# State-major tokens and 32-outermost stores for the sread MLP, and a later place for the sums and sread of batch 1

## The chip, the cores and the metric

One core of one Trainium2 chip. The metric is the device time of one execution in microseconds (us); the kernel before takes 229.64 us (median of the 4 runs that were made beside the changed kernel). Times "at 43.9" are us from the start of the span of the profile in question. Every profile is of one execution. The *tail* is the time from the start of TensorE's last matmul to the end of the span; the *handoff* is the passage of TensorE from batch 0 to batch 1.

## The reference, cut to what matters

```python
# x: (8 batches, 8 heads, 512, 64), state: (8, 8, 32, 64)
a     = softmax(scale * x @ state.T)            # over the 32 states
xread = a @ state                               # 512 tokens of each batch
a2    = softmax(scale * state @ x.T)            # over the 512 positions
sread = a2 @ x                                  # 32 tokens of each batch
tokens = concat([xread, sread], axis=2)  ->  (8 * 544, 512)
out = silu(tokens @ w_in) @ w_out               # w_in (512, 2048), w_out (2048, 512)
```

So the output has 8 blocks of 544 rows of 2 KB. The first 512 rows of a block come from xread and the last 32 from sread. The sread rows of all batches (8 x 32 = 256 tokens) are computed together, last, in two tiles of 128 tokens.

## The kernel before

In short: for each batch, `scores` (TensorE) and `exps` (ScalarE) make the exponentials; `norm` (VectorE, GpSimd) makes `an`, whose transpose is `aT`; `w1_chunks` folds the state into `w_in` (the tile W1). G1 is `aT` times W1, followed by SiLU on ScalarE; G2 is the second matmul, of 4 token tiles `tt` with 16 steps `ft` each. The tile `es` holds the token sums and `sread` uses it. All of this is interleaved by hand; each engine runs its instructions in program order.

```python
xpool = ctx.enter_context(tc.tile_pool(name="xpool", bufs=2))   # x_nat: x of a batch, bf16
banks = ["a0", "a1", "a2", "a3"]          # 4 PSUM banks taken in turn by scores, w1_chunks, sread, ...
xmT = pers.tile([128, 2, 4, 128], BF16)   # sread tokens: [feature, tile, kt, token]
out_sread = out.rearrange("(bb s) m -> bb s m", s=544)
# ... (cut)
def token_sums(b):                        # VectorE only
    f = att.tile([128, 2, 4, NS], FP32, tag="es_f", name="es_f")
    es[b] = att.tile([128, 2, 2, 4, NS], BF16, tag="es", name="es")
    for hg in range(2):
        nc.vector.tensor_reduce(f[:, hg], exp_nat[b, hg].rearrange("p c s n -> p s n c"), axis=AX, op=ADD)
    nc.vector.tensor_copy(es[b][:, 0], f[:])
    nc.vector.tensor_tensor(es[b][:, 1], f[:], es[b][:, 0], op=SUB)

def sread(b):                             # 18 matmuls, then VectorE
    ps = bank([128, 2, 4, 2, NS], FP32, "ps_sr")
    # ... (cut) 2 matmuls ones x es[b]; 16 matmuls x_nat[b] x exp_nat[b]
    nc.vector.reciprocal(rb[:], ps[:, 1, :, :, :])
    for g in range(2):
        for u in range(2):
            rows, k2 = ds(64 * u, 64), ds(2 * g, 2)
            nc.vector.tensor_tensor(
                xmT[rows, b // 4, k2, ds(32 * (b % 4), 32)],
                ps[rows, 0, k2, u ^ g, :], rb[rows, k2, u ^ g, :], op=MULT)
# ... (cut)
def last_half(b, tt, half):               # the last 128 tokens, 256 columns at a time
    # ... (cut) 16 matmuls, copy to o
    nc.sync.dma_start(out_sread[ds(4 * tt, 4), ds(512, 32), cols], o[:])
# ... (cut) end of batch 0: its last tile
for ft in range(NFT):
    if ft == 5:  w1_chunks(1, (3,), (nc.scalar, nc.scalar))
    if ft == 11:
        pe_transpose_a(1, 0, nc.scalar); pe_transpose_a(1, 1, nc.vector)
        # ... casts of x of batch 2, load of batch 3, transpose of x of batch 2
    if ft == 4:  token_sums(1)
    if ft == 13: sread(1)
    if ft >= 14: upto(NFT + ft - 12)      # first G1 of batch 1
    G2(0, 3, ft)
upto(NFT + 4)
store(0, 3, nc.vector)
for b in range(1, B):                     # n = b + 1: the batch that is prepared
    for tt in range(4):
        for ft in range(NFT):
            at = (tt, ft)
            # (0, 12): scores, exps of n          (1, 0): norm of n, casts of x of n+1, load of x of n+2
            # (1, 8): token_sums(n)               (2, 8): w1_chunks(n, (0, 1), both)
            # (3, 1), (3, 3), ...: G1 of n        (3, 4): w1_chunks(n, (2, 3), both)
            # (3, 8): DMA transpose of x of n+1   (3, 10): sread(n)
            G2(b, tt, ft)
        store(b, tt, nc.scalar if tt in (1, 2) else nc.vector)
# sread MLP: 16 steps of G1, G2; store(B, 0); last_half(B, 1, 0); last_half(B, 1, 1)
```

The softmax here doesn't subtract the row's maximum and nothing guards it: scores larger than these inputs give would overflow.

Of the kernel before, what the change touches and what calls it, by code (L numbers as in the profile page):

```python
# [9 lines left out]
BF16 = mybir.dt.bfloat16  # L10
# [11 lines left out]
NS = 32  # L22
# [14 lines left out]
def kernel(  # L37
# [8 lines left out]
    nc = tc.nc  # L46
    ds = bass.ds
# [3 lines left out]
    pers = ctx.enter_context(tc.tile_pool(name="pers", bufs=1))  # L51
# [14 lines left out]
    def bank(shape, dtype, name):  # L66
        tag = banks[turn[0] % len(banks)]
        turn[0] += 1
        return psA.tile(shape, dtype, tag=tag, name=name)
# [8 lines left out]
    ones = pers.tile([128, 128], BF16)  # L78
    w_in_sb = pers.tile([128, 4, DF], BF16)
    w_out_sb = pers.tile([128, NFT, DM], BF16)  # L80
    xmT = pers.tile([128, 2, 4, 128], BF16)

    win_re = moe_w_in.rearrange("(kt p) f -> p kt f", p=128)
    wout_re = moe_w_out.rearrange("(gg q) m -> q gg m", q=128)
    out_re = out.rearrange("(n4 four) m -> n4 four m", four=4)
    out_sread = out.rearrange("(bb s) m -> bb s m", s=544)


    x_nat = {}
# [30 lines left out]
    def copy(eng, dst, src):  # L120
        if eng is nc.scalar:
            nc.scalar.activation(dst, src, func=COPY, bias=0.0)  # L122
        else:
            eng.tensor_copy(dst, src)  # L124
# [158 lines left out]
    def pe_transpose_a(b, hg, eng):  # L283
        ps = bank([128, 4, 128], BF16, "ps_at")
        for c in range(4):
            nc.tensor.transpose(ps[:, c, :], an[b, hg][:, c, :, :], ident[:])
        copy(eng, aT[b][:, hg, :, :], ps[:])
# [4 lines left out]
    def token_sums(b):  # L292
# [3 lines that stand above are left out]
            nc.vector.tensor_reduce(  # L296
                f[:, hg], exp_nat[b, hg].rearrange("p c s n -> p s n c"), axis=AX, op=ADD
            )
        nc.vector.tensor_copy(es[b][:, 0], f[:])  # L299
        nc.vector.tensor_tensor(es[b][:, 1], f[:], es[b][:, 0], op=SUB)  # L300
# [3 lines left out]
    def sread(b):  # L304
        ps = bank([128, 2, 4, 2, NS], FP32, "ps_sr")
        for part in range(2):
            nc.tensor.matmul(  # L307
                ps[:, 1, :, :, :],
                ones[:],
                es[b][:, part],  # L310
                start=(part == 0),
                stop=(part == 1),
                skip_group_check=True,
            )
        for kt in range(4):
            for c in range(4):
                nc.tensor.matmul(  # L317
                    ps[:, 0, kt, :, :],
                    x_nat[b][:, c, ds(2 * kt, 2), :],
                    exp_nat[b, kt // 2][:, c, ds(2 * (kt % 2), 2), :],  # L320
                    start=(c == 0),
                    stop=(c == 3),
                    skip_group_check=True,
                )
        rb = att.tile([128, 4, 2, NS], FP32, tag="rb", name="rb")
        nc.vector.reciprocal(rb[:], ps[:, 1, :, :, :])  # L326
        for g in range(2):
            for u in range(2):
                rows, k2 = ds(64 * u, 64), ds(2 * g, 2)
                nc.vector.tensor_tensor(  # L330
                    xmT[rows, b // 4, k2, ds(32 * (b % 4), 32)],
                    ps[rows, 0, k2, u ^ g, :],
                    rb[rows, k2, u ^ g, :],
                    op=MULT,
                )
# [27 lines left out]
    def w1_chunks(b, fbs, engs):  # L363
        w1_cols(b, [(512 * fb, 512) for fb in fbs], engs)
# [6 lines left out]
    def emit_G1(k):  # L371
        b, ft = divmod(k, NFT)
        ps = psH.tile([128, 512], FP32, tag="h1", name="h1")
        if b < B:
            for hg in range(2):
                nc.tensor.matmul(  # L376
                    ps[:],
                    W1[b][:, hg, ds(128 * ft, 128)],
                    aT[b][:, hg, :, :],
                    start=(hg == 0),  # L380
                    stop=(hg == 1),
                    skip_group_check=True,
                )
        else:
            for kt in range(4):
                nc.tensor.matmul(  # L386
                    ps[:, 0:256],
                    w_in_sb[:, kt, ds(128 * ft, 128)],
                    xmT[:, :, kt, :],
                    start=(kt == 0),  # L390
                    stop=(kt == 3),
                    skip_group_check=True,
                )
        n = 512 if b < B else 256
        g = gpool.tile([128, 512], BF16, tag="g", name="g")
        gt[k] = g
        nc.scalar.activation(g[:, 0:n], ps[:, 0:n], func=SILU, bias=0.0)
# [16 lines left out]
    def store(b, tt, eng):  # L414
        o = opool.tile([128, DM], FP32, tag="o_sb", name="o_sb")
        copy(eng, o[:], outs[tt][:])
        if b < B:
            nc.sync.dma_start(out_re[ds(136 * b, 128), tt, :], o[:])
        else:
            nc.sync.dma_start(out_sread[ds(4 * tt, 4), ds(512, 32), :], o[:])  # L420


    def last_half(b, tt, half):
        cols = ds(DM // 2 * half, DM // 2)
        ps = bank([128, DM], FP32, "o_half")
        for ft in range(NFT):
            nc.tensor.matmul(  # L427
                ps[:, 0 : DM // 2],
                gt[b * NFT + ft][:, ds(128 * tt, 128)],
                w_out_sb[:, ft, cols],  # L430
                start=(ft == 0),
                stop=(ft == NFT - 1),
                skip_group_check=True,
            )
        o = opool.tile([128, DM // 2], FP32, tag="o_half", name="o_half")
        copy(nc.vector, o[:], ps[:, 0 : DM // 2])
        nc.sync.dma_start(out_sread[ds(4 * tt, 4), ds(512, 32), cols], o[:])


    both = (nc.vector, nc.scalar)  # L440
# [2 lines left out]
    def upto(k):  # L443
        while done[0] < min(k, (B + 1) * NFT):
            emit_G1(done[0])
            done[0] += 1
# [72 lines left out]
    for ft in range(NFT):  # L519
        if ft == 5:  # L520
            w1_chunks(1, (3,), (nc.scalar, nc.scalar))
        if ft == 11:
            pe_transpose_a(1, 0, nc.scalar)
            pe_transpose_a(1, 1, nc.vector)
            for c in range(4):
                cast_x(2, nc.gpsimd, c, 1)
            load_x(3)
            transpose_x(2)
        if ft == 4:
            token_sums(1)  # L530
        if ft == 13:
            sread(1)
        if ft >= 14:
            upto(NFT + ft - 12)
        G2(0, 3, ft)
# [3 lines left out]
    for b in range(1, B):  # L539
        n = b + 1  # L540
        lead = 4 if b == 1 else 6
        for tt in range(4):
            for ft in range(NFT):
                at = (tt, ft)
                if tt == 0:
                    upto(NFT * b + min(lead + ft, NFT))
                if n < B:
                    if at == (0, NFT - lead):
                        scores(n, 0)
                        scores(n, 1)  # L550
                        exps(n, 0)
                        exps(n, 1)
                        nc.scalar.activation(warm[:], warm[:], func=SILU, bias=0.0)  # L553
                    if at == (1, 0):
                        for hg in range(2):
                            norm(n, hg)
                            transpose_a(n, hg)
                        if n + 1 < B:
                            for c in range(4):
                                cast_x(n + 1, nc.gpsimd, c, 1)  # L560
                        if n + 2 < B:
                            load_x(n + 2)
                    if at == (1, 8):
                        token_sums(n)
                    if at == (3, 8):
                        if n + 1 < B:
                            transpose_x(n + 1)
                    if at == (3, 10):
                        sread(n)
                    if at == (2, 8):  # L570
                        w1_chunks(n, (0, 1), both)
                    if at == (3, 4):
                        w1_chunks(n, (2, 3), both)
                    if tt == 3 and ft % 2 == 1 and ft // 2 < 6:
                        upto(NFT * n + ft // 2 + 1)
                elif tt > 0 and (ft % 3 == 2 or ft == NFT - 1):
                    upto(min(done[0] + 1, NFT * (B + 1)))
# [3 lines that stand above are left out]
            gt.pop(NFT * b + ft)  # L581
# [34 lines left out]
```

## Time and profile before

| | before |
|---|---|
| time, median of the 3 runs at hand then | 229.88 us |
| span of the profile | 228.3 us |
| TensorE (PE) busy | 213.5 us, 94% |
| start of the last matmul to end of span (the tail) | 7.4 us |

The page of the kernel before gives the span, and the busy time of each engine with its share of the span (PEld are the weight loads):

```profile
span 228.3 us, 3733 instructions
...
PE 213.5 (94%) x1462; PEld 102.4 (45%) x1488; DVE 103.2 (45%) x186; ACT 142.5 (62%) x241; POOL 45.8 (20%) x64
...
PE 88%; DVE 6%; issue 1%; ACT 1%; POOL 0%; POOLq 0%
```

The last line is the chain that ended last, by engine. It says that TensorE is what is waited for. (It shows no DMA; the landings of the last three stores are missing from this trace.) How much of it could go is not to be read from the 94%. The Trainium skill ("Perfetto Trace Analysis", section "Identifying the Most-Contended Engine") warns that matmul busy time is no good measure of the distance to the limit. What can be read is where TensorE stands still.

*The tail.* The windows of the kernel before give, for each stretch of one us, its length, the busy time of PE, PEld, DVE, ACT and POOL (with the count of instructions), the granted clock, the mean busy share of the 16 DMA engines, and what they moved in GB/s:

```profile
216.00:217.00 1.00, 1.00 (x6) 0.48 (x5) 0.00 (x0) 0.00 (x0) 0.00 (x0) 1.00 0.58 217
...
220.00:221.00 1.00, 1.00 (x12) 0.84 (x9) 0.00 (x0) 0.00 (x0) 0.00 (x0) 1.00 0.28 14
221.00:222.00 1.00, 0.22 (x2) 0.00 (x0) 0.42 (x1) 0.00 (x0) 0.00 (x0) 1.00 0.20 49
...
223.00:224.00 1.00, 0.00 (x0) 0.00 (x0) 0.00 (x0) 0.00 (x0) 0.00 (x0) 1.00 0.27 101
...
226.00:227.00 1.00, 0.00 (x0) 0.00 (x0) 0.00 (x0) 0.00 (x0) 0.00 (x0) 0.50 0.19 66
```

The last matmuls, in the timeline of the kernel before (start, duration; the tail is counted from the start of the last of the 32, 220.95):

```profile
217.56 3.66 PE L427 MATMUL o_half<-w_out_sb,g 128*128 128x256 bf16 x32
```

From 222 on nothing computes; the kernel waits for its last stores. An ordinary store (216 to 217) moves 217 GB/s. The sread stores move about 100 GB/s at a share of 0.27, which is about 4 of 16 engines.

*The end of batch 0.* The waits of TensorE in the kernel before (who waited for whom: us in total, times, longest):

```profile
PE ps_sr L307 <- DVE es L299: 1.2, 1, 1.2
...
PE ps_sr L307 <- DVE es L300: 0.5, 1, 0.5
```

And the timeline of the kernel before there (start, duration, engine, line, operation, output and inputs, shapes, count; in brackets the idle time before it and what ended it):

```profile
43.24 0.38 PE L405 MATMUL o<-w_out_sb,g 128*128 128x512 bf16 x1
43.35 0.60 ACT L122 ACTIVATE aT<-ps_at 128x512 bf16<-128x512 bf16 x1
...
44.83 0.28 PE L307 MATMUL ps_sr<-es,ones 128*128 128x256 bf16 x1 [1.21 <-DVE es L299]
...
45.57 0.27 PE L307 MATMUL ps_sr<-es,ones 128*128 128x256 bf16 x1 [0.45 <-DVE es L300]
...
46.35 0.59 PE L376 MATMUL h_664<-aT,W_400 128*128 128x512 bf16 x2
```

The `sread` matmuls (L307, L317) stand in TensorE's order ahead of the first G1 of batch 1 (L376) and wait for the sums. Of what the G1 needs, `aT` comes last; it is there from 43.95.

*VectorE at the norm of batch 2*, in the timeline of the kernel before:

```profile
60.91 0.25 DVE L267 RECIPROCAL rc<-rs 128x16 f32<-128x16 f32 x1
61.08 1.91 DVE L296 TENSOR_REDUCE es_f<-exp_nat 128x128 f32<-128x512 bf16 x2
63.02 0.70 DVE L299 CAST es<-es_f 128x256 bf16<-128x256 f32 x1
63.75 0.71 DVE L300 TENSOR_TENSOR es<-es_f,es 128x256 bf16<-128x256 f32 x1
64.39 0.68 DVE L124 CAST W_848<-ps_w_849 128x512 bf16<-128x512 f32 x1
```

The first W1 copy of batch 2 (L124) ends at 65.07. The first G1 of batch 2, which reads it, starts at 65.59 without a wait:

```profile
65.59 0.59 PE L376 MATMUL h_886<-aT,W_848 128*128 128x512 bf16 x2
```

VectorE is packed here, and only half a microsecond is to spare.

### The profile page before, as it was taken

The numbers are of one execution on the slowest core, as the hardware profiler recorded it, in microseconds if no ns is written. First come the engines' busy times: TensorE is split into PE (matmuls) and PEld (weight loads), VectorE is DVE, ScalarE is ACT, GpSimd is POOL, SyncE is SP. The second block draws the span as 40 slices with busy tenths as digits, with TensorE's granted clock in tenths as the row PEclk, the third lists the DMA queues.
The fourth block names the chain that finished last, engine by engine and source line by source line (L and its number), as shares of the span: only waits on it lengthen the run. The fifth ranks groups of instructions, "written<-read, shape, count | busy, mean of one in ns | idle before, by whom it ended". The sixth has DMA issues, their size and how long they took to land.

```text
span 228.3 us, 3733 instructions
## 1 busy us (share of the span) xinstructions
PE 213.5 (94%) x1462; PEld 102.4 (45%) x1488; DVE 103.2 (45%) x186; ACT 142.5 (62%) x241; POOL 45.8 (20%) x64
## 2 busy tenths in 40 slices
PE   7799899799999999999999999999999999999970
PEld 2534335344435443544354534444444444566550
DVE  5554946960765075516552565247434634100110
ACT  2555558679865985598558856885679477444110
POOL 8380001710450045003600260025001200000000
PEclk9999999999999999999999999999999999999997
DMA  6999974585169115911591159113611311111111
GB/s 191 184 196 196 204 226 140 184 199 126 51 128 275 56 48 130 284 46 50 112 296 51 49 121 283 61 46 92 141 47 46 95 46 46 46 49 41 51 24 68
DMA packets 33933, 26.97 MB, mean 118 GB/s; under 512 B 22012, under 2 KB 27900, under 8 KB 33916
## 3 DMA queue, kind: packets, MB, share of 16 engines
q1 hardware_dynamic: 27244, 15.21, 25.6%
q0 software_dynamic: 6672, 11.54, 22.6%
q8 instruction: 11, 0.18, 0.3%
q14 instruction: 6, 0.05, 0.1%
HBM read 17.30 MB, written 8.91 MB: 115 GB/s over the span
## 4 chain that ended last, share of the span: by engine, by line
PE 88%; DVE 6%; issue 1%; ACT 1%; POOL 0%; POOLq 0%
PE o L405 46%; PE ps_sc L244 2%; PE ps_sr L317 2%; PE o_half L427 2%; PE ps_xt L185 1%; PE ps_busy L130 1%; PE o_a L405 1%; DVE rs L266 1%; DVE es_f L296 1%; PE ps_sr L307 1%; DVE rb L326 1%; DVE W_214 L124 1%; ACT exp_nat L256 1%; ACT xT_143 L122 1%; DVE x_nat_141 L101 0%
## 5 line engine op out<-in xcount | busy, mean ns | idle before, releaser
L405 PE MATMUL o<-w_out_sb,g 128*128 128x512 bf16 x489 | 132.1, 380 | 0.5
L405 PEld LDWEIGHTS <-g 128*128 128x128 bf16 x528 | 50.0, 98 | 58.6 <-issue 7.1
L124 DVE COPY o_sb<-o 128x512 f32<-128x512 f32 x17 | 11.8, 692 | 64.4 <-PE o L405 64.1
L269 POOL TENSOR_TENSOR an<-exp_nat,rc 128x512 bf16<-128x512 bf16 (+1 forms) x16 | 15.9, 1009 | 111.2 <-DVE rc L267 111.0
L326 DVE RECIPROCAL rb<-ps_sr 128x256 f32<-128x256 f32 x8 | 14.1, 1758 | 16.6 <-PE ps_sr L317 16.6
L122 ACT ACTIVATE o_sb<-o 128x512 f32<-128x512 f32 x15 | 8.9, 596 | 13.5 <-PE o L405 5.3
L296 DVE TENSOR_REDUCE es_f<-exp_nat 128x128 f32<-128x512 bf16 x16 | 15.3, 1000 | 0.0
L266 DVE TENSOR_REDUCE rs<-exp_nat 128x16 f32<-128x512 bf16 x16 | 10.6, 660 | 2.2 <-ACT exp_nat L256 1.5
L96 POOL DMA_DIRECT2D x_f<-in_x_dram x7 | 6.5, 924 | 20.6 <-DVE x_nat_486 L101 19.1
L256 ACT ACTIVATE exp_nat<-ps_sc 128x512 bf16<-128x512 f32 x16 | 8.8, 595 | 1.1 <-PE ps_sc L244 1.0
L386 PEld LDWEIGHTS <-w_in_sb 128*128 128x128 bf16 x64 | 6.3, 98 | 3.9
L256 ACT ACT_TABLE_LOAD x6 | 7.7, 1283 | 0.1
L553 ACT ACT_TABLE_LOAD x6 | 7.7, 1283 | 0.1
L330 DVE TENSOR_TENSOR xmT<-ps_sr,rb 64x64 bf16<-64x64 f32 x32 | 7.1, 222 | 0.6
L350 PEld LDWEIGHTS <-stT 64*32 64x32 bf16 x264 | 2.8, 89 | 9.1 <-issue 8.5
L130 PE MATMUL ps_busy<-busy 128*128 128x512 bf16 x11 | 5.4, 627 | 1.4 <-DVE busy L144 1.2
L405 PE MATMUL o_a<-w_out_sb,g 128*128 128x512 bf16 x15 | 5.8, 396 | 0.1
L376 PEld LDWEIGHTS <-W_214 128*128 128x128 bf16 x32 | 3.2, 106 | 5.1 <-DVE W_214 L124 1.5
L300 DVE TENSOR_TENSOR es<-es_f,es 128x256 bf16<-128x256 f32 x8 | 5.1, 638 | 0.3
L376 PEld LDWEIGHTS <-W_400 128*128 128x128 bf16 x32 | 3.1, 98 | 3.9 <-issue 0.3
L307 PE MATMUL ps_sr<-es,ones 128*128 128x256 bf16 x16 | 3.2, 273 | 1.7 <-DVE es L299 1.2
L376 PEld LDWEIGHTS <-W_1420 128*128 128x128 bf16 x32 | 3.1, 98 | 3.6 <-issue 0.2
(518 smaller groups left out, 351.1 us busy)
## 6 DMA issues: line engine op xcount, KB each, us to landing
out_dram<-o_sb SPq DMA_DIRECT2D x33, 256.0 KB, 2.4
x_f<-in_x_dram POOLq DMA_DIRECT2D x7, 1024.0 KB, 7.0
w_in_sb<-in_moe_w_in_dram POOLq DMA_DIRECT2D x3, 512.0 KB, 11.5
w_out_sb<-in_moe_w_out_dram POOLq DMA_DIRECT2D x3, 512.0 KB, 14.1
x_f<-in_x_dram SPq DMA_DIRECT2D x2, 512.0 KB, 4.4
st_f<-in_state_dram SPq DMA_DIRECT2D x8, 64.0 KB, 11.3
w_in_sb<-in_moe_w_in_dram POOLq DMA_DIRECT2D x2, 256.0 KB, 7.6
w_out_sb<-in_moe_w_out_dram POOLq DMA_DIRECT2D x2, 256.0 KB, 8.2
```

The costliest lines, as they stand in the source:

```text
L122: nc.scalar.activation(dst, src, func=COPY, bias=0.0)
L124: eng.tensor_copy(dst, src)
L130: nc.tensor.matmul(ps[:], busy[:, 0:128], busy[:], start=True, stop=True, skip_group_check=True)
L256: nc.scalar.activation(e[:], sc_ps[hg][:], func=EXP, bias=0.0, scale=SCALE)
L266: nc.vector.tensor_reduce(rs[:], e[:], axis=AX, op=ADD)
L269: eng.tensor_tensor(a[:, ds(c, n)], e[:, ds(c, n)], rc[:, ds(c, n)].to_broadcast([128, n, 4, NS]), op=MULT,)
L296: nc.vector.tensor_reduce(f[:, hg], exp_nat[b, hg].rearrange("p c s n -> p s n c"), axis=AX, op=ADD)
L326: nc.vector.reciprocal(rb[:], ps[:, 1, :, :, :])
L330: nc.vector.tensor_tensor(xmT[rows, b // 4, k2, ds(32 * (b % 4), 32)], ps[rows, 0, k2, u ^ g, :], rb[rows, k2, u ^ g, :], op=MULT,)
L376: nc.tensor.matmul(ps[:], W1[b][:, hg, ds(128 * ft, 128)], aT[b][:, hg, :, :], start=(hg == 0), stop=(hg == 1), skip_group_check=True,)
L405: nc.tensor.matmul(outs[tt][:], gt[b * NFT + ft][:, ds(128 * tt, 128)], w_out_sb[:, ft, :], start=(ft == 0), stop=(ft == NFT - 1), skip_gr ...
L553: nc.scalar.activation(warm[:], warm[:], func=SILU, bias=0.0)
```

## The change

Its intent: (1) order the 256 sread tokens by state first and batch second, so that the 3-dimensional stores have 32 rows outermost instead of 4, and more DMA engines share the last stores; (2) take the sums and the sread of batch 1 out of TensorE's way at the end of batch 0.

```diff
-    xmT = pers.tile([128, 2, 4, 128], BF16)
+    xmT = pers.tile([128, 2, 4, NS, 4], BF16)
-    out_sread = out.rearrange("(bb s) m -> bb s m", s=544)
+    out_sread = out.rearrange("(bb s) m -> s bb m", s=544)
@@ sread: the four products
-                    xmT[rows, b // 4, k2, ds(32 * (b % 4), 32)],
+                    xmT[rows, b // 4, k2, :, b % 4],
@@ G1 of the sread MLP
-                    xmT[:, :, kt, :],
+                    xmT[:, :, kt].rearrange("p t n b -> p t (n b)"),
@@ store, last_half (there with cols)
-            nc.sync.dma_start(out_sread[ds(4 * tt, 4), ds(512, 32), :], o[:])
+            nc.sync.dma_start(out_sread[ds(512, 32), ds(4 * tt, 4), :], o[:])
@@ last tile of batch 0
-        if ft == 4:
-            token_sums(1)
-        if ft == 13:
-            sread(1)
@@ loop over batches, tt == 0 / tt == 1
                     upto(NFT * b + min(lead + ft, NFT))
+                    if b == 1 and ft == 2:
+                        token_sums(1)
+                if b == 1 and at == (1, 4):
+                    sread(1)
```

More of the change, by code (lines that the diff above doesn't have):

```diff
@@ L436, in last_half @@
         copy(nc.vector, o[:], ps[:, 0 : DM // 2])
-        nc.sync.dma_start(out_sread[ds(4 * tt, 4), ds(512, 32), cols], o[:])
+        nc.sync.dma_start(out_sread[ds(512, 32), ds(4 * tt, 4), cols], o[:])
     both = (nc.vector, nc.scalar)
```

## The prediction

> **What bounds the kernel now.** TensorE. The page gives PE 213.5 us of 228.3 busy (94%), granted clock 0.994, and PE is 88% of the chain that ended last. The change touches two places without PE work.
>
> 1. *The tail.* In the timeline the last PE work ends near 221.3 and the last eviction at 221.67; the span ends at 228.3. The three sread stores are issued at 218.38, 219.96 and 221.71. By one-microsecond windows DMA runs there at 95 to 101 GB/s with a busy share of 0.27, about 4 of 16 engines; SyncE's last landing wait ends near 227.4, and 0.97 us of closing barrier follows. An ordinary store (issued 215.03, same 256 KB) reached 217 GB/s and landed 2.05 us after issue.
> 2. *Batch 0 to 1.* The waits view has PE waiting 1.2 us for the first half of the token sums and 0.5 us for the second. The chain of waits passes through DVE there.
>
> **The stores.** The Trainium skill ("DMA: Bandwidth & Descriptors", section on why a semaphore rises by 16) says a DMA uses the largest count up to 16 that divides the slowest dimensions of both sides. Before it is 4 (batches), after it is 32 (state rows) against 128 partitions, so 16. The trace agrees for before: 4 x 2048 B/85 ns = 96 GB/s. After, each store should land about 1.9 us after issue (issue 0.54 us, 8 packets of 1 KB at 46 ns per engine, write receipt; estimate from the ordinary store). The last one lands near 223.6 instead of 227.4: **-3.7 us**, all on the critical path. The strided xmT writes (222 ns each) should cost the same.
>
> **The moved sums and sread.** Removed at the handoff: from the G2 matmul at 43.24 the next one starts at 46.14. After the change the first G1 matmul waits only for the aT copy of ScalarE (ends 43.95), so it starts near 44.0 instead of 46.35: **-2.35 us**. Given back: the sread matmuls run later, **+0.7** (2 x 0.11 + 0.47, as at 70.5). Then a new wait: VectorE is packed from 59.2 to 65.7 (norm of batch 2, its sums, two W1 evictions); the moved reciprocal (1.76) and four products (0.93) enter ahead of the sums. The first W1 eviction of batch 2, now ending at 65.07, ends about 2.4 us later, while PE, which wants it at 65.6, arrives only 0.7 later: **+1.2** before the first G1 of batch 2. Scores of batch 2 come 2.35 us earlier, near 54.1; their transposed x ends its packets at 53.5: 0 to 0.3 us more. Sum of this part: about **-0.4** (-1.3 to +0.3).
>
> Total -4.1: 229.9 to about **225.7 us**, 8 in 10 between **225.0 and 226.6**. Chances: faster by over 2% 0.27, within 2% 0.71, slower 0.02.
>
> **What would show it.** Tail: DMA share over 0.5 in the windows of the sread stores and 3.3 us from PE's last matmul to the span's end. Handoff: no PE wait for es; first G1 of batch 1 near 44.0. Batch 1: PE waits around 65 (after's time) for VectorE's W1 copy, about 1.2 us.
>
> **What would make it wrong.** The stores still on 4 engines: only -0.4 in all. VectorE's eviction not delayed as I think (or PE reaching it later): up to -5.3, over 2% faster. The pool's cast of batch 3 waiting for the late sread (same x buffer), or a later scores wait: less gain.

## The result

The changed kernel takes 226.26 us (225.40 to 226.91, 4 runs) against 229.64 (229.19 to 230.03, 4 runs). The ratio is 0.9849, 95% interval 0.9815 to 0.9883: 1.5% faster, inside the 2% that counts as the same. Ratios here and below are the mean time of one kernel's fast runs over that of the other's of the same rounds, so they are not quite the ratio of the medians quoted. The predicted 225.7 us is 0.6 us too low.

The page of the changed kernel, the lines that answer to those of before:

```profile
span 224.7 us, 3733 instructions
...
PE 213.9 (95%) x1462; PEld 102.2 (45%) x1488; DVE 104.8 (47%) x186; ACT 142.5 (63%) x241; POOL 45.5 (20%) x64
...
PE 80%; DVE 9%; DMA 4%; issue 2%; POOL 2%; ACT 1%; POOLq 0%; DVEq 0%
```

The windows of the changed kernel's tail (same columns), and its last matmuls:

```profile
220.00:221.00 1.00, 1.00 (x11) 0.79 (x9) 0.00 (x0) 0.00 (x0) 0.00 (x0) 1.00 0.35 129
221.00:222.00 1.00, 0.17 (x2) 0.00 (x0) 0.42 (x1) 0.00 (x0) 0.00 (x0) 1.00 0.39 131
222.00:223.00 1.00, 0.00 (x0) 0.00 (x0) 0.00 (x0) 0.00 (x0) 0.00 (x0) 1.00 0.12 41
223.00:224.70 1.70, 0.00 (x0) 0.00 (x0) 0.00 (x0) 0.00 (x0) 0.00 (x0) 0.95 0.16 53
```

```profile
217.51 3.66 PE L427 MATMUL o_half<-w_out_sb,g 128*128 128x256 bf16 x32
```

The stores no longer pile up. By the trace each lands 2.1 to 2.5 us after its issue: the last is issued at 221.66 and lands at 223.72, and the span ends 1.0 us later. In the kernel before, SyncE's waits for the three stores ended at 224.7, 226.0 and 227.4, the last one 5.7 us after its issue (221.71).

TensorE's waits in the changed kernel:

```profile
PE h L376 <- DVE W L124: 1.3, 2, 1.1
```

The waits for `es` are gone, and a wait for VectorE's W1 copy is new. The timeline of the changed kernel at the end of batch 0, then at the scores of batch 2, then at the first G1 of batch 2:

```profile
43.11 0.81 PE L405 MATMUL o<-w_out_sb,g 128*128 128x512 bf16 x2
43.22 0.60 ACT L122 ACTIVATE aT<-ps_at 128x512 bf16<-128x512 bf16 x1
...
43.87 1.02 PE L376 MATMUL h<-aT,W 128*128 128x512 bf16 x4
...
54.29 0.41 PEld L244 LDWEIGHTS <-xT 128*128 128x128 bf16 x12 [0.63 <-DMA xT<-x_nat]
...
65.43 0.61 PE L376 MATMUL h<-aT,W 128*128 128x512 bf16 x2 [1.09 <-DVE W L124]
```

The first G1 of batch 1 now starts 2.5 us earlier. But the first G1 of batch 2 (65.43 here, 65.59 before) starts hardly earlier. VectorE's timeline in the changed kernel shows why:

```profile
58.68 0.25 DVE L267 RECIPROCAL rc<-rs 128x16 f32<-128x16 f32 x1
58.85 1.69 DVE L326 RECIPROCAL rb<-ps_sr 128x256 f32<-128x256 f32 x1
60.58 1.25 DVE L330 TENSOR_TENSOR xmT<-ps_sr,rb 64x64 bf16<-64x64 f32 x4
61.86 2.00 DVE L296 TENSOR_REDUCE es_f<-exp_nat 128x128 f32<-128x512 bf16 x2
63.89 0.29 DVE L299 CAST es<-es_f 128x256 bf16<-128x256 f32 x1
64.22 0.43 DVE L300 TENSOR_TENSOR es<-es_f,es 128x256 bf16<-128x256 f32 x1
64.68 1.29 DVE L124 CAST W<-ps_w 128x512 bf16<-128x512 f32 x2
```

The reciprocal (L326) and the products (L330) of the moved sread now stand ahead of the sums and the W1 copies. The products write with strides now; the pages give their busy time and the mean ns of one, first in the kernel before, then in the changed kernel:

```profile
L330 DVE TENSOR_TENSOR xmT<-ps_sr,rb 64x64 bf16<-64x64 f32 x32 | 7.1, 222 | 0.6
...
L330 DVE TENSOR_TENSOR xmT<-ps_sr,rb 64x64 bf16<-64x64 f32 x32 | 9.6, 300 | 0.6
```

To compare kernels I cut each profile into stretches between matmuls that all of them have: the first scores matmul (L244) of batches 1, 2, 3 and 7, the first G1 of batch 2, and the start of the last matmul. All are starts read from the timelines, and the differences are mine. Up to the scores of batch 1 all kernels have the same instructions (only where the four products of batch 0 write differs with the layout).

```text
us from ... to ...             start to    b1 to     b1 to first  b1 to     b3 to     b7 to last  last matmul
                               scores b1   scores b2 G1 of b2     scores b3 scores b7 matmul      to end
before                         38.97       17.51     26.62        40.31     92.95     48.71       7.41
changed                        38.83       15.46     26.59        40.30     93.05     48.71       3.82
e1 stores only                 39.86       17.51     26.62        40.32     93.10     48.71       3.79
e2 move only                   38.67       15.43     26.26        39.96     92.95     48.71       7.47
e3 changed, again              39.01       15.51     26.64        40.35     93.02     48.71       3.81
e4 sread early                 37.07       15.91     25.04        38.73     92.95     48.71       3.78
e5 eight batches outermost     37.77       17.52     26.63        40.32     92.95     48.71       4.35
e7 one batch per transfer      38.53       17.51     26.63        40.32     93.15     48.72       4.98
e8 sread after W1              38.15       15.45     25.99        41.43     92.96     48.71       3.79
e9 e8 with three x buffers     39.31       15.43     26.68        40.38     93.47     48.72       3.79
e10 e4 again                   38.87       15.92     25.05        38.74     93.43     48.71       3.81
```

Two things are to be read here. First, the same instructions took 37.1 to 39.9 us to the scores of batch 1, so the spans of two profiles cannot be compared to better than 2 to 3 us; the stretches behind that point repeat to a few hundredths where nothing was changed, apart from the long one from batch 3 to batch 7, which varied by 0.5. That variation lies in one place: from the scores of batch 4 to those of batch 5 it took 23.24 us in the runs where the two transposing DMAs of `aT` of batch 4 needed up to 4.62 us from the first issue to the last landing, 23.31 to 23.44 where they needed 4.75 to 4.87 (the changed kernel, e3, e1, e7), and 23.72 and 23.76 where they needed 5.15 and 5.19 (e10, e9). Why these DMAs vary is not shown. Second, the change gained 3.59 us in the last column and nothing between the scores of batches 1 and 3. My theory A after this reading was: the whole gain is the stores, and the move nets to nothing because VectorE's queue and the transposed x give its gain back. The rival, B: the move earns a part of it and the stores less.

### The profile page after: what moved, and what is told of

Same layout as the page of the kernel before. It is cut to its first block, busy times and chain, and to the rows that moved or that the text cites. A ratio compares the mean times of both kernels' runs of the same rounds, so it can differ in the third digit from the quotient of the medians.

```text
span 224.7 us, 3733 instructions
## 1 busy us (share of the span) xinstructions
PE 213.9 (95%) x1462; PEld 102.2 (45%) x1488; DVE 104.8 (47%) x186; ACT 142.5 (63%) x241; POOL 45.5 (20%) x64
## 4 chain that ended last, share of the span: by engine, by line
PE 80%; DVE 9%; DMA 4%; issue 2%; POOL 2%; ACT 1%; POOLq 0%; DVEq 0%
PE o L405 42%; PE h L376 22%; DMA xT<-x_nat 4%; PE ps_w L350 4%; PE h L386 3%; PE ps_sc L244 2%; DVE es_f L296 2%; PE o_half L427 2%; DVE rb L326 2%; PE ps_sr L317 1%; PE ps_xt L185 1%; PE ps_busy L130 1%; DVE rs L266 1%; DVE W L124 1%; POOL x_nat L101 1%
## 5 line engine op out<-in xcount | busy, mean ns | idle before, releaser
L397 ACT ACTIVATE g<-h 128x512 bf16<-128x512 f32 (+1 forms) x144 | 82.2, 573 | 44.3 <-PE h L376 30.0
L376 PE MATMUL h<-aT,W 128*128 128x512 bf16 x256 | 76.5, 383 | 1.8 <-DVE W L124 1.3
L376 PEld LDWEIGHTS <-W 128*128 128x128 bf16 x256 | 24.9, 98 | 31.9 <-DVE W L124 3.1
L124 DVE CAST W<-ps_w 128x512 bf16<-128x512 f32 (+1 forms) x31 | 20.0, 676 | 18.4 <-PE ps_w L350 18.3
L122 ACT ACTIVATE W<-ps_w 128x512 bf16<-128x512 f32 (+1 forms) x35 | 18.7, 575 | 9.4 <-PE ps_w L350 9.3
L326 DVE RECIPROCAL rb<-ps_sr 128x256 f32<-128x256 f32 x8 | 14.0, 1750 | 16.2 <-PE ps_sr L317 16.2
L101 POOL CAST x_nat<-x_f 128x512 bf16<-128x512 f32 x24 | 14.7, 646 | 0.0
L350 PE MATMUL ps_w<-w_in_sb,stT 64*32 64x512 bf16 (+1 forms) x264 | 11.5, 383 | 0.0
L330 DVE TENSOR_TENSOR xmT<-ps_sr,rb 64x64 bf16<-64x64 f32 x32 | 9.6, 300 | 0.6
L386 PE MATMUL h<-xmT,w_in_sb 128*128 128x256 bf16 x64 | 9.6, 273 | 0.0
```

What stands on the lines that cost most here:

```text
L101: eng.tensor_copy(x_nat[b][:, ds(c0, nc_), ds(h0, nh), :], x_f[:, ds(h0, nh), ds(c0, nc_), :].rearrange("p h c d -> p c h d"),)
L122: nc.scalar.activation(dst, src, func=COPY, bias=0.0)
L124: eng.tensor_copy(dst, src)
L350: nc.tensor.matmul(pss[f, hg][ds(32 * s, 32), 0:n], stT[ds(r, 64), b, h // 2, s % 2, :], w_in_sb[ds(r, 64), h // 2, ds(f, n)], start=True, ...
L376: nc.tensor.matmul(ps[:], W1[b][:, hg, ds(128 * ft, 128)], aT[b][:, hg, :, :], start=(hg == 0), stop=(hg == 1), skip_group_check=True,)
L386: nc.tensor.matmul(ps[:, 0:256], w_in_sb[:, kt, ds(128 * ft, 128)], xmT[:, :, kt].rearrange("p t n b -> p t (n b)"), start=(kt == 0), stop ...
```

## The experiments

### e1 and e2: the two halves of the change by themselves

The diffs are the first four hunks of the change (e1) and its last two (e2).

> Only the state-major layout and the 32-outermost stores; sums and sread of batch 1 stay where they were. Theory A (the whole gain is the tail, the move nets to nothing because its 2.35 us come back as sread work 0.7, a VectorE wait of 1.1 and a DMA wait of 0.6): time 3.6 to 3.8 us below before, so equal to the change within 0.3 us; last landing about 2 us after the last issue. Theory B (the move earns a part, the stores less than 3 us): 1 us or more slower than the change. The four strided products should take about 300 ns each instead of 222 without any PE wait for them.

e1: 225.89 us (225.20 to 227.76, 6 runs), ratio to before 0.9856 (0.9819 to 0.9893). Tail 3.79 us; the stretch b1 to b3 is 40.32 us, as in before. The products took 299 ns each and nothing waited for them.

> Only the move of the sums and sread of batch 1; layout and stores as before. Theory A: within 0.4 us of before (0 to 0.4 us faster, because the products with contiguous writes take 0.93 instead of 1.25 us and shorten the VectorE wait before the first G1 of batch 2 from 1.1 to about 0.8 us); the waits for es are gone, the waits for the W1 copy and for the transposed x of batch 2 stand in their place. Theory B: 1 us or more faster than before.

e2: 228.96 us (228.50 to 229.99, 6 runs), ratio 0.9983 (0.9954 to 1.0012). The stretch b1 to b3 is 0.35 us shorter than in before. The waits for `es` are gone; the wait for the W1 copy stands in their place, and the weight loads of the scores of batch 2 wait 0.6 us for the transposed x, as theory A had it:

```profile
PE h L376 <- DVE W L124: 0.9, 1, 0.9
```

So the stores alone give what the change gives, and the move alone gives nothing that the times can show. B is refuted. The move's stretch differs by 0.34 us with the layout (39.96 in e2, 40.30 in the changed kernel), which is what four products of 300 instead of 222 ns cost (4 x 78 ns = 0.31 us).

### e3: the changed kernel on the same chip

> The changed kernel as it is, on the same chip as the others, so that the others can be compared with it: 226.0 to 226.5 us, 1.5% under before.

226.93 us (225.78 to 227.48, 6 runs), ratio 0.9883 (0.9851 to 0.9914), 0.4 us over the range that I had given. Its stretches equal those of the first profile within 0.06 us, except for the start (0.17 us).

### e4: sread of batch 1 early in the first quarter

```diff
-                if b == 1 and at == (1, 4):
+                if b == 1 and at == (0, 6):
                     sread(1)
```

> The changed kernel with sread of batch 1 at step 6 of the first quarter of its MLP instead of step 4 of the second. VectorE is idle there from 49.4 to 55.8 us in the changed kernel, es is ready at 49.35 and this step comes at about 50. Theory A: the VectorE wait before the first G1 of batch 2 (1.1 us) disappears, and the 0.7 us of sread work come ahead of the scores of batch 2, so that most of their 0.6 us wait for the transposed x is filled: 1.3 to 1.7 us faster than the changed kernel, about 224.7 us. Rival (the PE stretch there is paced by ScalarE or the VectorE wait only moves elsewhere): less than 0.5 us faster than the changed kernel.

224.21 us (223.28 to 224.98, 5 runs), ratio 0.9768 (0.9738 to 0.9798), which is faster by over 2%. The stretch b1 to b3 is 38.73 us, 1.57 less than in the changed kernel, and the first G1 of batch 2 comes 1.55 us sooner after the scores of batch 1. The timeline of e4 shows VectorE doing the moved work in its idle time, and then TensorE starting that G1 without a wait:

```profile
49.22 1.76 DVE L326 RECIPROCAL rb<-ps_sr 128x256 f32<-128x256 f32 x1 [1.63 <-PE ps_sr L317]
51.01 1.24 DVE L330 TENSOR_TENSOR xmT<-ps_sr,rb 64x64 bf16<-64x64 f32 x4
...
62.10 0.59 PE L376 MATMUL h<-aT,W 128*128 128x512 bf16 x2
```

Theory A holds, the rival does not. The time fell by 2.7 us against e3 (medians), more than the 1.6 us of the stretch. In the two profiles the start differs by 1.9 us as well (37.07 and 39.01); that this scatter also makes up the rest in the medians is likely, but not shown.

### e5: the dose, 8 outermost

Tokens are ordered as half of the states, then the 8 batches, then 16 states (from before, shortened; the place of sums and sread is before's):

```diff
+    xmT = pers.tile([128, 2, 4, B, 16], BF16)
+                    xmT[rows, :, k2, b, :],          # ps and rb split alike, "p k (t n) -> p t k n"
+            nc.sync.dma_start(out_sread[:, ds(512 + 16 * tt, 16), :], o[:])
```

> Before's place of sums and sread; tokens ordered as half of the states, then 8 batches, then 16 states, so that each sread store has 8 batches outermost, batch rows together as before. A dose between 4 and 32. Theory A (the tail is set by how many DMA engines the outermost size admits, here 8): from the start of PE's last matmul to the span's end 4.2 to 4.8 us (4 engines 7.4, 16 engines 3.8), issue to landing of the last half store 1.9 to 2.4 us (16 engines 2.06). Rival (what matters is that neighbouring rows of the output are written far apart, as state-major does): as before, over 7 us. The four products, whose runs are now 32 bytes long, should take 222 to 240 ns each if it is the run length of 2 bytes that costs 300.

226.06 us (225.94 to 226.79, 4 runs), ratio 0.9866 (0.9845 to 0.9887). It was run on another chip. The tail is 4.35 us, between 7.41 (4 outermost) and 3.82 (32). Landings of these stores are not in the record of this run, so that expectation can't be read; the last data packet ended 2.28 us after the last issue (5.33 in the kernel before, 1.71 in the changed one). The products took 222 ns again. Windows of e5 in its tail:

```profile
219.00:220.00 1.00, 1.00 (x10) 0.68 (x7) 0.00 (x0) 0.00 (x0) 0.00 (x0) 1.00 0.41 72
220.00:221.00 1.00, 0.03 (x1) 0.00 (x0) 0.42 (x1) 0.00 (x0) 0.00 (x0) 1.00 0.49 177
```

8 of 16 engines, all busy, would be a share of 0.50.

### e7: before's rows and partitions, one transfer per batch

```diff
-            nc.sync.dma_start(out_sread[ds(4 * tt, 4), ds(512, 32), :], o[:])
+            for i in range(4):
+                nc.sync.dma_start(out_sread[4 * tt + i, ds(512, 32), :], o[ds(32 * i, 32), :])
```

(and the same in `last_half`).

> Before's layout and order, but each sread store is issued as four transfers, one batch of 32 partitions and 32 consecutive rows each, so the rows go where and from where they did and the outermost size is 32. Theory A (engines): all 16 engines take part and the data itself is as fast as in the change; what is left is the issue of four times as many transfers, 0.33 to 0.54 us each: from PE's last matmul to the span's end 4.4 to 5.4 us. Rival (address order): over 7 us.

226.87 us (226.21 to 227.67, 4 runs), ratio 0.9885 (0.9862 to 0.9909). The tail is 4.98 us. Issues follow each other every 0.46 us, and the last lands 1.56 us after its issue. Every row goes from the same partition to the same address as before, and the tail is 2.4 us shorter: it is not the order of the addresses. What is left over against the change is the four issues in a row.

### e8 and e9: sread behind the W1 matmuls

```diff
-                if b == 1 and at == (1, 4):
-                    sread(1)
                     if at == (2, 8):
                         w1_chunks(n, (0, 1), both)
+                        if b == 1:
+                            sread(1)
```

> The changed kernel with sread of batch 1 behind the first W1 matmuls of batch 2 (step 8 of the third quarter), so its reciprocal and products queue behind the W1 copies on VectorE and behind the sums of batch 2, while its PE work stays behind the scores. It takes away the VectorE wait alone. Theory A: the wait of the first G1 of batch 2 for the W1 copy (1.1 us) is gone, the wait of the scores for the transposed x (0.6 us) stays: the stretch from the scores of batch 1 to the scores of batch 3 is 39.1 to 39.5 us (40.3 in the changed kernel and in before, 38.7 with the early sread). A wait of up to 0.5 us for a PSUM bank before the second pair of W1 chunks may come in. Rival (the wait is for something else than VectorE's queue): 40.0 us or more.

A miss: 227.76 us (226.90 to 228.44, 4 runs), ratio 0.9932 (0.9902 to 0.9961), and 41.43 us from b1 to b3 instead of 39.1 to 39.5. The wait of the first G1 of batch 2 for the W1 copy did go (25.99 us from b1 to that G1, against 26.59). But two new waits came. TensorE's waits in e8:

```profile
PE ps_sc L244 <- DMA xT<-x_nat: 1.6, 1, 1.6
...
PE ps_sr L307 <- DVE W L124: 0.7, 1, 0.7
```

The timeline of GpSimd (POOL) in e8, which waited for the sread matmuls before its cast:

```profile
62.43 2.29 POOL L101 CAST x_nat<-x_f 128x512 bf16<-128x512 f32 x4 [2.86 <-PE ps_sr L317]
65.01 0.93 POOL L96 DMA_DIRECT2D x_f<-in_x_dram  x1 [0.30 <-POOL x_nat L101]
```

sread took a PSUM bank that the W1 copies had yet to free (0.7 us). And the cast of x of batch 3 takes the buffer of x of batch 1, so it waited for the late sread. The next load of x was then issued at 65.01 and the transposing DMA of batch 3 at 65.18 (62.76 and 65.22 in the changed kernel), and that transpose landed 14.4 us after issue instead of 6.7. The scores of batch 3 waited for it.

To test that, e9 gives x three buffers:

```diff
-    xpool = ctx.enter_context(tc.tile_pool(name="xpool", bufs=2))
+    xpool = ctx.enter_context(tc.tile_pool(name="xpool", bufs=3))
```

> The kernel with sread behind the W1 matmuls, but with three buffers for the x of a batch instead of two, so that the casts of batch 3 need not wait for the late sread. Theory (the 1.6 us wait of the scores of batch 3 came from that wait: the casts ended late, the next load of x and the transposing DMA were issued together and the transpose landed 14 instead of 7 us after issue): that wait disappears, and from the scores of batch 1 to those of batch 3 it takes 39.6 to 40.1 us (41.4 with two buffers). Rival (the scores wait for something else): 41 us or more.

227.09 us (226.79 to 227.60, 4 runs), ratio 0.9901 (0.9873 to 0.9930). It was run on another chip. The wait of the scores is gone, so the buffer was its cause. The stretch is 40.38 us, 0.3 over the range that I had given. The wait for the bank grew by 0.7 us, and the first G1 of batch 2, which stands behind it, came 0.69 us later than in e8 (26.68 against 25.99):

```profile
PE ps_sr L307 <- DVE W L124: 1.4, 1, 1.4
```

In e9 the casts of GpSimd run at the time of VectorE's sums again, and the sums' cast and subtraction take 0.71 and 0.71 us there. In e8, with GpSimd waiting, they took 0.29 and 0.43.

### e10: the early sread once more

> The kernel with the early sread again, on another turn on the chip, to settle its gain over before: the stretch between the scores of batches 1 and 3 should be 38.7 us again, and the time 224.2 to 225.0 us, which is 3.6 us of tail plus 1.6 us of that stretch under before (229.5).

225.45 us (225.17 to 225.58, 5 runs), ratio 0.9824 (0.9798 to 0.9850); the interval spans the 2%, so by itself this turn leaves it unclear whether the gain is over 2%. The stretch b1 to b3 is 38.74 us again and the tail 3.81. The time is 0.45 us over the range that I had given; in its profile 0.48 us of that lies between the scores of batches 3 and 7 (93.43 against 92.95 in e4), where the two kernels are the same: all of it between the scores of batches 4 and 5, where TensorE waited 0.3 us for the transposed `aT` of batch 4. Its two DMAs took 5.15 us from the first issue to the second landing, against 4.62 in e4, which has no such wait. Between its two turns on the chip the early sread is 1.8 to 2.3% faster than before. It is the best version that I found, 0.8 to 2.7 us under the changed kernel by the medians (225.45 and 224.21 against 226.26 and 226.93; of these only 224.21 and 226.93 are of the same rounds), and 1.6 us by the stretch.

## Why the prediction was right, point by point

- *The tail.* Predicted -3.7 us, measured -3.59 (7.41 to 3.82). The mechanism, more engines on each store, holds. The Trainium skill ("DMA: Bandwidth & Descriptors", section "Why a DMA increments its semaphore by 16 and not by 1") says that a transfer uses the largest number of DMA engines up to 16 that divides the outermost sizes of both sides. With 4, 8 and 32 outermost against 128 partitions the tail was 7.41, 4.35 and 3.82 us; the busy share agreed with the rule for 4 engines (0.27 of 16) and for 8 (up to 0.49). e7 excludes the order of the addresses. My sign "share over 0.5 in the windows" fails in windows of one us, which show 0.35 to 0.39, because the stores are so short; a window of 0.4 us at the first of them (219.60 to 220.00) shows 0.88 and 333 GB/s. One part I had not foreseen: about 1.9 of the 7.3 us that the stores of the kernel before took are their slow beginning (7.3 against 5.4, above), not the rate of 4 engines, and it is gone with 16. My forecast held because it was the difference between a measured landing and an estimated one; it did not explain that part.
- *The handoff.* Predicted -2.35 us. The first G1 of batch 1 starts 5.04 us after the first scores matmul of batch 1 (43.87 - 38.83), before it was 7.38 (46.35 - 38.97): -2.34.
- *The transposed x.* Predicted 0 to 0.3 us more; the gain at the scores of batch 2 is 2.05 instead of 2.34 us, so 0.29. I had called the wait small from the last packet; the landing at 54.25 decided it.
- *The moved sread matmuls.* Predicted +0.7 us, measured 0.69 (56.49 to 57.18).
- *The W1 copy.* Predicted +1.2 us, measured 1.09. (A wait is counted from the end of the matmul before it, 0.38 us after its start; in a row they start about 0.21 us apart. So TensorE lost about 1.26 us; this is an estimate.) e4 takes the wait away and gains. The size is luck in part: from the start of the norm of batch 2 to the end of the first W1 copy it was 5.85 us (59.22 to 65.07) and is 8.38 (56.99 to 65.37), 2.5 us more where I had 2.4. But the reciprocal and products took 3.0 us instead of my 2.7, and the cast and subtraction behind them gave back 0.6 (last two points).
- *The products.* I said that the strided writes "should cost the same". They cost 300 instead of 222 ns. This is the step that failed, and with it the sum of the move: predicted -0.4, measured -0.01, still within my range of -1.3 to +0.3. With contiguous writes (e2) the move gives -0.35. The products are slow in all 8 batches, but in e1, with the old order, nothing waited for them; only behind the norm of batch 2, where VectorE has no slack, do the 0.31 us reach TensorE. It is a small term, and the forecast of the whole stood in spite of it: 226.26 lies between 225.0 and 226.6, and the change is within 2%.
- *The sums' cast and subtraction* of batch 2 went the other way than the products, and I had not counted on it fully: 0.29 and 0.43 us instead of 0.70 and 0.71. They now run after GpSimd's casts of x (60.19 to 62.46) instead of beside them. The Trainium skill ("SBUF — State Buffer", section "Who interferes with whom") says that a VectorE instruction with two SBUF inputs contends with a GpSimd instruction that reads SBUF. The subtraction agrees in every run looked at: 0.71 us beside the casts (before, e4, e9, e10) and 0.43 us without them (the changed kernel, e2, e8). The cast has one SBUF input, so that sentence does not cover it; it slowed with the subtraction all the same. No run was made for this point; it is read from the timing alone.

What stays open: why the start of the kernel scatters by up to 2.8 us with the same instructions, and why the first stores on 4 engines begin so slowly (see the end). No run was spent on either. The traces place a part of the scatter before the first scores matmul of batch 0 (at 6.71 us in e4, 7.84 in e1); most of it comes later.

## What to carry to other kernels

The last store of a kernel is fully exposed, so look at its outermost dimension: a layout that puts 32 rows outermost, where only 4 stood, halved a tail of 7.4 us at almost no cost. Work that is moved off one engine's path lands in another engine's queue and holds buffers there; look for the stretch in which that engine has idle time (here step 6 instead of step 20 of the same loop, worth 1.6 us), and follow what its input buffers and PSUM banks hold up. And compare kernels between matmuls that both have, not by spans: here the start alone scattered by up to 2.8 us, nearly the effect of the whole change.

## What the Trainium skill lacked or had wrong

- "DMA: Bandwidth & Descriptors": its rule for the number of engines agrees with the busy shares of the sread stores here (0.27 with 4 engines, up to 0.49 with 8, 0.88 in 0.4 us with 16). It says nothing of the slow beginning of stores on few engines: with 4, the engines were busy as later (share 0.28 of 16) but moved 14 GB/s from 220 to 221 us and 101 GB/s from 223 on; with 8 (e5), 72 and then 177 GB/s; with 16 (the changed kernel), 133 GB/s in the first window, at a share of 0.35, and its first packets took 85 ns each from the start, as the later ones did, where with 4 some took 400 to 990 ns. The cause is open.
- "SBUF — State Buffer", section "Door 1": it says that full bandwidth needs at least two hits in each 16-byte line, and gives 8 bf16 elements as how far one can stride for free (it does not say for which engine). VectorE's products of 64x64 elements took 300 ns when they wrote one bf16 element in every 4 (2 bytes every 8, so two in each 16) and 222 ns when they wrote runs of 32 or 64 bytes. So for these writes the stride was not free.
- No page that I read gives a figure for a transposing DMA that is issued together with a load on another queue: it landed 14.4 us after issue when the load was issued 0.17 us earlier (e8), 9.2 us after it when the load was issued 1.4 us earlier (e10), and 6.7 us after it with 2.5 us between them (the changed kernel). It is one case of each kind, apart from e4, which agrees with e10 (9.2 us at 1.4 us); the transpose of batch 2, issued 0.27 us ahead of a load, took 9.2 us in the changed kernel.
